# First batch's keys in three parts instead of two, scored two steps behind, and a shorter choice of its expert

## The chip, the core and the metric

The kernel runs on one core of a Trainium2 chip. The metric is the device time of one execution in microseconds (us), as the median of several runs. Five engines matter: TensorE (PE, its weight loads are PEld), VectorE (DVE), ScalarE (ACT), GpSimd (POOL) and SyncE (SP), which issues nearly all transfers. Each engine takes its instructions in the order in which the program was laid out. That layout is made when the program is compiled: a planner takes the order of the source as the order of priority and moves an instruction ahead where its inputs and its buffer are free.

## The reference

Four batches of 10048 tokens with 128 channels, 49 agents, 16 experts (4 groups of 4) with 1024 hidden units.

```python
a2k = softmax(scale * agents @ k.T)      # 49 x 10048, per batch
agent_v = a2k @ v                        # 49 x 128
x = softmax(scale * q @ agents.T) @ agent_v
g = argmax(x @ w_group); e = argmax(x @ w_expert[g])
out = p(g) * p(e | g) * (relu(x @ w1[g, e]) @ w2[g, e])
```

The values of a token depend on all keys of its batch, through `agent_v`. So no token of the first batch can go through an expert before all of that batch's keys and values have been read.

## The kernel before, in words

Keys, values and queries come in chunks of 8 tiles of 128 tokens: ten chunks to a batch, the last one of 7 tiles (the seventh of 64 rows). The program handles batch 1 first, then 2, 3 and 0 (`PB`). It has three pieces in time:

- **The front**, lines 424 to 529, runs alone before anything else. It reads the first batch's keys and values, forms `agent_v`, picks the expert that most of the batch's tokens will take (the main expert) and starts to load its weights.
- **The experts.** Lines 1239 to 1266 pass tile after tile of 512 tokens through the main expert, batch after batch. Beside them run "lanes", the same attention work for the later batches and the routing of this one, which are advanced by how far the experts have come.
- **The rest**: tokens of the last batch that take another expert are gathered, computed and scattered.

In the front the order of the work around the keys is a string, `ORDER` (line 68): `k` loads and splits the next key chunk, `m` takes the maximum over the chunks since the last `m`, `v` takes the exponentials of the next chunk and issues its value load, `q` runs the whole of query chunk 0. Scores and value products always run one step behind.

A key chunk goes like this. `load` (214) brings 512 KB into one of four `xf` buffers. `split_load` (224) makes a high half `xh` on ACT and the rest `xl` on DVE, or on POOL in four pieces where `POOLED` (69) has a 1: chunks 1, 4 and 7. Both halves come from a pool `wk` with two buffers each. `key_scores` (272) issues 24 matmuls, three for each tile of 128 keys, copies the bank to `S` on ACT and takes the maximum over the tiles from `S` on DVE (285). `key_max` (291) is a chain between two engines: reduce the chunk maxima (`mx`), transpose on PE, reduce again (`ma`), multiply into a diagonal (`dg`), spread over all partitions by a matmul with ones, copy to `mb`. `key_exp` (318) subtracts `mb` on DVE, takes the exponential on ACT and issues the value load (`vf`, six buffers). `key_values` (336) multiplies the exponentials with the values in fp32, two matmuls in the trace for each tile of 128 keys, into one PSUM bank. That bank holds one sum for each of the two parts; `agents_done` (468) scales and adds them and divides, which gives `av`.

`main_soon` (751) then chooses the main expert from the sum of the tokens: two small matmuls and eleven DVE instructions from `msum` to `mainid`. `load_weights` (812) reads `mainid` into a register of SP and issues the loads `w1f` and `w2f`. `agents_scaled` (496) scales `av` into `at`: transpose, reduction and reciprocal on one partition, and a matmul with ones that spreads the result. `at` multiplies `w1f` in `weights_of` (824), which the first expert tile needs, and makes `rh` for the routing.

```python
ORDER = "kkkkkmkvkvkvkvkvmqvvvvv"
POOLED = "0100100100"
```

Of the kernel before, what the change touches and what calls it, by code (L numbers as in the profile page):

```python
# [11 lines left out]
F16 = mybir.dt.float16  # L12
I32 = mybir.dt.int32
AF = mybir.ActivationFunctionType
ALU = mybir.AluOpType
# [5 lines left out]
P = 128  # L21
B = 4
N = 10048
C = 128
# [42 lines left out]

ORDER = "kkkkkmkvkvkvkvkvmqvvvvv"
POOLED = "0100100100"
RANGES = [(0, CT), (CT, 3 * CT), (3 * CT, 5 * CT), (5 * CT, 7 * CT), (7 * CT, NTP)]  # L70
# [62 lines left out]
def build(ctx, tc, qT, kT, v, agT, wr, w1, w2, cpk, out):  # L133
# [90 lines left out]
    def split_load(kind, b, ci, early=None):  # L224
        t0, t1 = chunks[ci]
        n = (t1 - t0) * P if kind == "q" else min(N, t1 * P) - t0 * P
        xf = loaded.pop((kind, b, ci), None)
        if xf is None:
            xf = load(kind, b, ci)
        xh = wk.tile([P, CT * P], F16, name="xh", tag="xh")  # L230
        xl = wk.tile([P, CT * P], F16, name="xl", tag="xl")
        act.activation(xh[:, 0:n], xf[:, 0:n], AF.Copy)
        if early and POOLED[ci] == "0":
            vec.tensor_sub(out=xl[:, 0:n], in0=xf[:, 0:n], in1=xh[:, 0:n])
        else:
# [35 lines left out]

    def key_scores(b, ci):

# [10 lines left out]
        act.activation(S[:, t0:t0 + full], ps[:, 0:full * NA].rearrange("p (t a) -> p t a", a=NA), AF.Copy)  # L284
        vec.tensor_reduce(out=mch[:, ci], in_=S[:, t0:t0 + full].rearrange("p t a -> p a t"), axis=AX.X, op=ALU.max)
        if t1 == NT:
# [4 lines left out]
    def key_max(b, c0, c1, early):  # L291
# [12 lines left out]
        vec.tensor_reduce(out=ma, in_=ps[0:NA, 0:P], axis=AX.X, op=ALU.max)  # L304
        dg = sm.tile([NA, NA], F32, name="dg")
        vec.tensor_scalar(out=dg, in0=identf[0:NA, 0:NA], scalar1=ma, scalar2=None, op0=ALU.mult)
        yield
        ps = bank(b)
        pe.matmul(ps[:, 0:NA], ones[0:NA, :], dg, start=True, stop=True)
        yield  # L310
        mb = sm.tile([P, 1, NA], F32, name="mb")
        vec.tensor_copy(out=mb[:, 0], in_=ps[:, 0:NA])
        if i == 0 and early:
            st["acc"] = bank(1)
        st["part"].append((c0, c1, mb, st["acc"][0:NA, i * (C + 1):(i + 1) * (C + 1)] if early else None))
        yield

    def key_exp(b, i, ci, early):

        S, mb = state[b]["S"], state[b]["part"][i][2]  # L320
        t0, t1 = chunks[ci]
        for a, z, m in ((t0, min(t1, NT - 1), P), (NT - 1, t1, LAST)):
            if z <= a:
                continue
            vec.tensor_sub(out=S[0:m, a:z], in0=S[0:m, a:z], in1=mb[0:m].broadcast_to([m, z - a, NA]))
            act.activation(S[0:m, a:z], S[0:m, a:z], AF.Exp)
        vf = early.tile([P, CT, C + 1], F32, name="vf", tag="vf", bufs=6)
        nf = min(t1, NT - 1) - t0
# [95 lines left out]
    def front(b, early, order):  # L424

        first = queries_of(b, early, [0])
        behind, part, at, done = None, {}, {"k": 0, "v": 0}, 0
        for x in order:
            if x == "q":
                yield from first  # L430
                continue
            if x == "m":
                if behind:
                    yield from behind
                behind = None
                yield from key_max(b, done, at["k"], True)
                for c in range(done, at["k"]):
                    part[c] = len(state[b]["part"]) - 1
                done = at["k"]
                continue  # L440
            c = at[x]
            at[x] += 1
            if x == "k":
                yield from key_load(b, c, early)
            else:
                yield from key_exp(b, part[c], c, early)
            if behind:
                yield from behind
            behind = key_scores(b, c) if x == "k" else key_values(b, part[c], c)
        if behind:  # L450
            yield from behind
# [16 lines left out]
    def agents_done(b, early):  # L468

        st = state[b]  # L470
        acc, *other = [x[3] for x in st["part"]]
        if other:
            n = len(st["part"])
            mm = early.tile([NA, 1], F32, name="mm")
            vec.tensor_reduce(out=mm, in_=st["ma"][:, 0:n], axis=AX.X, op=ALU.max)
            wt = early.tile([NA, n], F32, name="wt")
            vec.tensor_scalar(out=wt, in0=st["ma"][:, 0:n], scalar1=mm, scalar2=None, op0=ALU.subtract)
            act.activation(wt, wt, AF.Exp)
            a0 = early.tile([NA, C + 1], F32, name="a0")
            vec.tensor_scalar(out=a0, in0=acc, scalar1=wt[:, 0:1], scalar2=None, op0=ALU.mult)  # L480
            for i, x in enumerate(other):
                vec.scalar_tensor_tensor(out=a0, in0=x, scalar=wt[:, i + 1:i + 2], in1=a0, op0=ALU.mult, op1=ALU.add)
            acc = a0
        za = sm.tile([NA, 1], F32, name="za")
        vec.tensor_scalar(out=za, in0=acc[:, C:C + 1], scalar1=1e-9, scalar2=None, op0=ALU.add)
        vec.reciprocal(out=za, in_=za)
        av = sm.tile([NA, C], F32, name="av")
        vec.tensor_scalar(out=av, in0=acc[:, 0:C], scalar1=za, scalar2=None, op0=ALU.mult)
# [5 lines left out]
        yield from agents_scaled(b, psT[:, 0:NA])  # L494

    def agents_scaled(b, avT):
# [254 lines left out]
    def main_soon(b, early, av):  # L751

        st = state[b]
        row = lambda n, name: sm.tile([1, n], F32, name=name)
        su, g, e, o, m = row(NG + NE, "msum"), row(1, "mg"), row(1, "me"), row(NG, "mog"), row(NE, "mm")
        ps = bank(b)
# [7 lines left out]
        yield  # L764
        vec.tensor_copy(out=su, in_=ps[0:1, 0:NG + NE])
        vec.tensor_reduce(out=g, in_=su[:, 0:NG], axis=AX.X, op=ALU.max)
        vec.tensor_reduce(out=e, in_=su[:, NG:], axis=AX.X, op=ALU.min)
        vec.tensor_scalar(out=o, in0=su[:, 0:NG], scalar1=g, scalar2=None, op0=ALU.is_ge)
        vec.tensor_scalar(out=m, in0=su[:, NG:], scalar1=e, scalar2=None, op0=ALU.subtract)
        vec.tensor_mul(out=m.rearrange("p (g e) -> p g e", g=NG), in0=m.rearrange("p (g e) -> p g e", g=NG),  # L770
                       in1=o.unsqueeze(2).broadcast_to([1, NG, 4]))
        vec.tensor_reduce(out=g, in_=m, axis=AX.X, op=ALU.max)
        vec.scalar_tensor_tensor(out=m, in0=m, scalar=g, in1=rev[0:1], op0=ALU.is_ge, op1=ALU.mult)
        vec.tensor_reduce(out=g, in_=m, axis=AX.X, op=ALU.max)
        vec.tensor_scalar(out=e, in0=g, scalar1=-1.0, scalar2=float(NE - 1), op0=ALU.mult, op1=ALU.add)
        mi = sm.tile([1, 1], I32, name="mainid")
        vec.tensor_copy(out=mi, in_=e)
        st["mainid"], st["maine"] = mi, e
        yield

    def main_row(b):

        st = state[b]
        ps = bank(b)
        pe.matmul(ps[:, 0:1], ones[0:1, :], st["maine"], start=True, stop=True)
        yield
# [507 lines left out]
```

## Time and profile before

| | |
|---|---|
| median of 3 runs | 1002.93 us (998.78 to 1003.92) |
| the profiled execution's own time | 1004.48 us |
| its span, first to last instruction | 1002.6 us |
| mean granted clock of TensorE | 0.975 of full speed |
| busy: PE, DVE, ACT, POOL | 922.4, 770.3, 639.9, 474.1 us |
| read from HBM, written | 89.01 MB, 33.75 MB |

All times below are us from the span's start. Busy time of PE is the time with a matmul in the pipe, so matmuls that overlap count once. In the granted clock 1.00 stands for 2.4 GHz and 0.50 for 1.2 GHz, the two levels. In a timeline row the second number runs from the start of the first instruction of a merged row to the end of the last one; the number in brackets is the idle time before it and who ended it.

### The profile page before, as it was taken

To read this page: it belongs to the slowest core of one execution; us is meant where nothing else is said; L and a number is where in the kernel's file an instruction comes from. 1 tells how busy PE (TensorE), PEld (TensorE's weight loads), DVE (VectorE), ACT (ScalarE), POOL (GpSimd) and SP (SyncE) were. 2 spreads that over 40 slices of the span, in tenths; PEclk is the share of its full clock that TensorE was granted. 3 is DMA by queue.
4 is the path that set the end of the run, shared out by engine and by line. 5 is a ranking of instruction groups with operands and counts; after the bars stand their busy time and mean duration, and the time that the engine had idled before them with its cause. 6 is when DMAs were issued, how large, how long until landed. Compare 5 with 4: busy or idle time off the path is not lost.

```text
span 1002.6 us, 31456 instructions
## 1 busy us (share of the span) xinstructions
PE 922.4 (92%) x13192; PEld 733.5 (73%) x13192; DVE 770.3 (77%) x1477; ACT 639.9 (64%) x1144; POOL 474.1 (47%) x772
## 2 busy tenths in 40 slices
PE   3878998989998999999899989999999999999986
PEld 3756776767776777787677868877776777777765
DVE  5769879987698887868979766689998766666643
ACT  4537667688756787875677657865455655555542
POOL 2226347288304536730362255400003758888885
PEclk9879999999999999999999999999999999999988
DMA  9744236344037734301773332112422734343321
GB/s 280 231 138 132 80 103 206 95 141 120 23 118 252 203 97 124 103 24 36 240 258 107 110 96 62 33 36 75 161 70 94 251 116 157 125 125 117 117 71 43
DMA packets 104423, 124.58 MB, mean 124 GB/s; under 512 B 6743, under 2 KB 88152, under 8 KB 101328
## 3 DMA queue, kind: packets, MB, share of 16 engines
q1 hardware_dynamic: 99920, 116.57, 36.5%
q0 software_dynamic: 4352, 5.91, 2.2%
q8 instruction: 105, 1.72, 0.7%
q14 instruction: 46, 0.38, 0.1%
HBM read 89.01 MB, written 33.75 MB: 122 GB/s over the span
## 4 chain that ended last, share of the span: by engine, by line
PE 37%; DVE 13%; POOL 6%; issue 2%; ACT 2%; DMA 1%; POOLq 0%; SPq 0%; DVEq 0%; ACTq 0%
PE po L128 19%; PE ph L128 13%; DVE hl L128 6%; PE at L128 5%; POOL out L1111 2%; POOL er L1074 2%; POOL gap L1090 1%; POOL xl L238 1%; DVE oo L128 1%; DMA xf<-kT 1%; ACT hh L128 1%; DVE oh L128 1%; DVE oa L128 1%; DVE za L128 0%; ACT vh L128 0%
## 5 line engine op out<-in xcount | busy, mean ns | idle before, releaser
L128 DVE SCALAR_TENSOR_TENSOR hl<-ph,hh 128x512 f16<-128x512 f32 (+1 forms) x656 | 437.2, 678 | 143.8 <-ACT hh L128 141.0
L128 PEld LDWEIGHTS <-hh 128*128 128x128 f16 x5200 | 427.9, 98 | 150.7 <-issue 6.3
L128 ACT ACTIVATE hh<-ph 128x512 f16<-128x512 f32 (+1 forms) x656 | 382.6, 592 | 210.7 <-PE ph L128 205.4
L128 PE MATMUL po<-wbuf,hh 128*128 128x128 f16 x4816 | 476.4, 220 | 0.0
L128 PE MATMUL po<-wbuf,hl 128*128 128x128 f16 x2408 | 439.1, 220 | 0.0
L128 PE MATMUL ph<-et,wbuf 98*128 98x512 f16 (+1 forms) x1040 | 311.9, 380 | 20.9 <-DVE hl L128 20.5
L238 POOL TENSOR_TENSOR xl<-xf,xh 128x256 f16<-128x256 f32 (+1 forms) x288 | 191.9, 700 | 207.1 <-ACT xh L128 204.7
L128 PEld LDWEIGHTS <-hl 128*128 128x128 f16 x2600 | 254.9, 98 | 2.9 <-issue 0.3
L1074 POOL DMA_INDIRECT er<-erow,gidx x68 | 69.3, 1019 | 126.2 <-DVE over L128 113.1
L128 PEld LDWEIGHTS <-wbuf 98*128 98x128 f16 x1216 | 95.7, 99 | 32.4 <-issue 29.6
L128 ACT ACTIVATE xh<-xf 128x1024 f16<-128x1024 f32 x80 | 83.4, 1043 | 46.0 <-PE at L128 19.0
L380 POOL TENSOR_TENSOR sl<-S,sh 128x147 f16<-128x147 f32 (+1 forms) x90 | 46.0, 538 | 97.2 <-ACT sh L128 97.2
L1111 POOL DMA_INDIRECT out<-oo,sidx x68 | 67.7, 995 | 25.5 <-DVE oo L128 14.5
L590 POOL TENSOR_TENSOR rows<-ef,rows 128x147 f16<-128x147 f32 (+2 forms) x117 | 48.0, 437 | 50.0 <-ACT rows L128 49.8
L128 PEld LDWEIGHTS <-xh 128*128 128x128 f16 x1264 | 60.8, 100 | 14.3 <-ACT xh L128 12.8
L128 PE MATMUL at<-agh,xl 128*128 128x49 f16 x577 | 58.1, 187 | 8.8 <-POOL xl L238 8.8
L128 PEld LDWEIGHTS <-xl 128*128 128x128 f16 x632 | 53.3, 99 | 14.4 <-POOL xl L238 11.3
L128 PE MATMUL at<-agh,xh 128*128 128x49 f16 x577 | 58.3, 187 | 2.2 <-ACT xh L128 2.0
L128 PE MATMUL at<-agl,xh 128*128 128x49 f16 x577 | 57.9, 187 | 0.0
L128 PE MATMUL ph<-ets,wbuf 98*128 98x512 f16 x176 | 53.6, 388 | 0.0
L1090 POOL MEMSET gap<- 128x320 f16 x136 | 52.3, 384 | 0.3
L128 DVE TENSOR_TENSOR oo<-po,cw 128x512 f32<-128x512 f32 x65 | 43.7, 673 | 10.1 <-PE po L128 10.1
(281 smaller groups left out, 1061.5 us busy)
## 6 DMA issues: line engine op xcount, KB each, us to landing
xf<-kT SPq DMA_DIRECT2D x36, 512.0 KB, 4.3
vf<-v SPq DMA_DIRECT2D x36, 512.0 KB, 5.2
xf<-qT SPq DMA_DIRECT2D x36, 512.0 KB, 4.1
out<-oo SPq DMA_DIRECT2D x62, 256.0 KB, 2.5
wbuf<-wall SPq DMA_DIRECT2D x11, 1024.0 KB, 5.0
wsg<-wall SPq DMA_DIRECT2D x6, 1024.0 KB, 5.0
erow<-rows SPq DMA_DIRECT2D x3, 1975.0 KB, 7.7
w1f<-w SPq DMA_DIRECT2D x7, 512.0 KB, 5.5
```

The costliest lines, as they stand in the source:

```text
L128: return f(*a, **k)
L238: pool.tensor_sub(out=xl[:, y], in0=xf[:, y], in1=xh[:, y])
L380: pool.tensor_sub(out=sl[0:m, w], in0=x[:, j], in1=sh[0:m, w])
L590: (vec if early else pool).tensor_sub(out=rows[:, w, NA:2 * NA], in0=ef[:, y], in1=rows[:, w, 0:NA])
L1074: ins = pool.indirect_dma_start(out=er[:, q], out_offset=None, in_=erow[b][:, :], in_offset=bass.IndirectOffsetOnAxis(ap=place(b, j * w + ...
L1090: tc.keep_in_program_order(pool.memset(gap, 0.0))
L1111: ins = pool.indirect_dma_start(out=out, out_offset=bass.IndirectOffsetOnAxis(ap=place(x["b"], x["j"] * n + q)[1], axis=0), in_=o[:, q], i ...
```

## The change

`ORDER` becomes a list of sixty steps with separate letters for loading a key chunk (`l`), splitting it (`k`), scoring it (`s`), loading values (`V`), exponentials (`v`), products (`p`), loading the queries (`Q`) and one stage of query chunk 0 (`q`). Scores stand two splits behind. There are three `m`, after chunks 3, 6 and 9. Each step also advances the running maximum by one stage. Odd key chunks split into a second pair of buffers, and POOL splits chunks 1, 3, 6 and 8. The maximum of the tiles is read from PSUM. The third part's sum has a PSUM bank of its own. In `key_max` and in `agents_scaled` a matmul with a broadcast operand takes the place of the diagonal and of the one-partition step. The choice of the expert takes five DVE instructions and writes the index by `max_index`; the first reduction of `agents_scaled` is held behind it.

```diff
-ORDER = "kkkkkmkvkvkvkvkvmqvvvvv"
-POOLED = "0100100100"
+ORDER = ("l l l l k l k l k l s V k l s V k l s V k l s m k Q s V v s V v p s V v p m V k v p s V k p v s V k p v s V p m v p "
+         "v p q v p v p q q q").split()
+POOLED = "0101001010"
@@ split_load
-        xh = wk.tile([P, CT * P], F16, name="xh", tag="xh")
-        xl = wk.tile([P, CT * P], F16, name="xl", tag="xl")
+        xp = early if early and kind == "k" and ci % 2 else wk
+        xh, xl = [xp.tile([P, CT * P], F16, name=x, tag=x, bufs=2) for x in ("xh", "xl")]
@@ key_scores
-        vec.tensor_reduce(out=mch[:, ci], in_=S[:, t0:t0 + full].rearrange("p t a -> p a t"), axis=AX.X, op=ALU.max)
+        x = ps[:, 0:full * NA].rearrange("p (t a) -> p t a", a=NA) if early else S[:, t0:t0 + full]
+        vec.tensor_reduce(out=mch[:, ci], in_=x.rearrange("p t a -> p a t"), axis=AX.X, op=ALU.max)
@@ key_max
-        dg = sm.tile([NA, NA], F32, name="dg")
-        vec.tensor_scalar(out=dg, in0=identf[0:NA, 0:NA], scalar1=ma, scalar2=None, op0=ALU.mult)
         yield
         ps = bank(b)
-        pe.matmul(ps[:, 0:NA], ones[0:NA, :], dg, start=True, stop=True)
+        pe.matmul(ps[:, 0:NA], ma.broadcast_to([NA, P]), identf[0:NA, 0:NA], start=True, stop=True)
...
-        if i == 0 and early:
+        if early and i != 1:
             st["acc"] = bank(1)
-        st["part"].append((c0, c1, mb, st["acc"][0:NA, i * (C + 1):(i + 1) * (C + 1)] if early else None))
+        k = i % 2 * (C + 1)
+        st["part"].append((c0, c1, mb, st["acc"][0:NA, k:k + C + 1] if early else None))
@@ front
+        query = queries_of(b, early, [0])
+        next(query)
+        chain, part, at = iter(()), {}, dict.fromkeys("lksmVvp", 0)
...
         for x in order:
+            next(chain, None)
...
+            elif x == "m":
+                whole(chain)
+                chain = key_max(b, c and at["done"], at["s"], early)
+                for y in range(c and at["done"], at["s"]):
+                    part[y] = c
+                at["done"] = at["s"]
+                next(chain)
+            elif x == "V":
+                yield from key_values_load(b, c, early)
+            elif x == "v":
+                if part[c] >= len(st["part"]):
+                    whole(chain)
+                yield from key_exp(b, part[c], c)
+            elif x == "p":
+                yield from key_values(b, part[c], c)
+        whole(query)
@@ agents_scaled
-        vec.tensor_reduce(out=am, in_=avT, axis=AX.X, op=ALU.max, apply_absolute_value=True)
+        ins = vec.tensor_reduce(out=am, in_=avT, axis=AX.X, op=ALU.max, apply_absolute_value=True)
+        if pinned:
+            tc.keep_in_program_order(ins)
         yield
         ps = bank(b)
-        pe.transpose(ps[0:1, 0:P], am, identf)
-        yield
-        sc = sm.tile([1, 2], F32, name="sc")
-        vec.tensor_reduce(out=sc[:, 1:2], in_=ps[0:1, 0:P], axis=AX.X, op=ALU.max)
-        vec.tensor_scalar(out=sc[:, 1:2], in0=sc[:, 1:2], scalar1=1e-30, scalar2=1.0 / AMAX, op0=ALU.max, op1=ALU.mult)
-        vec.reciprocal(out=sc[:, 0:1], in_=sc[:, 1:2])
-        yield
-        ps = bank(b)
-        pe.matmul(ps[:, 0:2], ones[0:1, :], sc, start=True, stop=True)
+        pe.matmul(ps[:, 0:P], am.broadcast_to([P, P]), identf, start=True, stop=True)
         yield
         scb = sm.tile([P, 2], F32, name="scb")
-        vec.tensor_copy(out=scb, in_=ps[:, 0:2])
+        vec.tensor_reduce(out=scb[:, 1:2], in_=ps[:, 0:P], axis=AX.X, op=ALU.max)
+        vec.tensor_scalar(out=scb[:, 1:2], in0=scb[:, 1:2], scalar1=1e-30, scalar2=1.0 / AMAX, op0=ALU.max, op1=ALU.mult)
+        vec.reciprocal(out=scb[:, 0:1], in_=scb[:, 1:2])
@@ main_soon, in place of the eleven instructions of lines 765 to 777
+        g, o, m = row(1, "mg"), row(NG, "mog"), row(NE, "mm")
+        vec.tensor_reduce(out=g, in_=ps[0:1, 0:NG], axis=AX.X, op=ALU.max)
+        vec.tensor_scalar(out=o, in0=ps[0:1, 0:NG], scalar1=g, scalar2=1.0, op0=ALU.is_ge, op1=ALU.subtract)
+        vec.scalar_tensor_tensor(out=m.rearrange("p (g e) -> p g e", g=NG), in0=o.unsqueeze(2).broadcast_to([1, NG, 4]), scalar=3e38,
+                                 in1=ps[0:1, NG:NG + NE].rearrange("p (g e) -> p g e", g=NG), op0=ALU.mult, op1=ALU.add)
+        best = row(8, "best")
+        which = sm.tile([1, 8], U32, name="which")
+        vec.max(out=best, in_=m)
+        vec.max_index(out=which, in_max=best, in_values=m)
+        st["mainid"] = which.bitcast(I32)
```

`agents_done` adds three parts in the place of two, by one more DVE instruction of the kind at line 482; `key_values_load` is the second half of `key_exp` (lines 327 to 334) as a step of its own; `main_row` casts the index back to a float.

## Rows read from the trace of the kernel before

**Rows 1.** Busy time by stage: stretch, length, PE, PEld, DVE, ACT, POOL, clock, DMA, GB/s
```profile
0.00:63.00 63.00, 41.29 (x478) 36.53 (x479) 35.14 (x99) 25.08 (x40) 15.14 (x25) 0.93 0.67 204
...
83.00:100.00 17.00, 14.66 (x199) 11.40 (x198) 16.84 (x45) 11.80 (x24) 9.54 (x18) 1.00 0.39 123
...
300.00:400.00 100.00, 94.11 (x1451) 75.02 (x1449) 83.28 (x137) 76.37 (x135) 50.82 (x85) 0.98 0.56 169
```

**Rows 2.** Timeline of ACT, 0 to 62: splits, what each waited for
```profile
11.06 1.06 ACT L128 ACTIVATE xh<-xf 128x1024 f16<-128x1024 f32 x1 [1.23 <-PE po L128]
...
24.24 1.06 ACT L128 ACTIVATE xh<-xf 128x1024 f16<-128x1024 f32 x1 [3.59 <-PE ph L128]
25.20 0.48 ACT L128 ACTIVATE S<-ph 128x392 f32<-128x392 f32 x1
...
32.92 0.90 ACT L128 ACTIVATE xh<-xf 128x832 f16<-128x832 f32 x1 [2.02 <-PE at L128]
```

**Rows 3.** Timeline of PE, 24 to 58: value products, maximum, query chunk 0
```profile
26.26 5.80 PE L128 MATMUL at<-vf,S 128*49 128x129 f32 x32 [0.81 <-ACT S L128]
...
32.70 1.97 PE L128 MATMUL at<-vf,S 128*49 128x129 f32 x16
...
40.15 0.31 PE L128 MATMUL at<-cp,mx 128*49 128x128 f32 x1 [0.31 <-DVE mx L128]
...
43.35 0.87 PE L128 MATMUL at<-vf,S 128*49 128x129 f32 x6 [1.70 <-ACT S L128]
44.06 1.34 PE L128 MATMUL ph<-ones,ef 128*49 128x1 f32 x16
...
49.01 7.92 PE L128 MATMUL at<-vf,S 128*49 128x129 f32 x60
```

**Rows 4.** Timeline of DVE, 22 to 62: both maxima, agents, choice of expert
```profile
22.16 0.57 DVE L128 TENSOR_REDUCE mx<-mch 128x49 f32<-128x245 f32 x1
...
23.60 0.24 DVE L128 TENSOR_SCALAR dg<-cp,ma 49x49 f32<-49x49 f32 x1
...
24.83 0.21 DVE L128 COPY mb<-at 128x49 f32<-128x49 f32 x1 [0.97 <-PE at L128]
...
29.05 0.81 DVE L128 TENSOR_REDUCE mch<-S 128x49 f32<-128x392 f32 x1
...
30.28 1.21 DVE L128 TENSOR_TENSOR xl<-xf,xh 128x1024 f16<-128x1024 f32 x1
...
39.52 0.57 DVE L128 TENSOR_REDUCE mx<-mch 128x49 f32<-128x245 f32 x1
...
56.97 0.34 DVE L128 TENSOR_SCALAR a<-at,wt 49x129 f32<-49x129 f32 x1 [7.43 <-PE at L128]
...
59.37 0.17 DVE L128 COPY msum<-po 1x20 f32<-1x20 f32 x1
...
61.62 0.13 DVE L128 CAST mainid<-me 1x1 int32<-1x1 f32 x1
```

**Rows 5.** Busy time, 39 to 51: the second maximum and the products behind it
```profile
39.00:44.00 5.00, 2.92 (x41) 2.38 (x40) 4.19 (x13) 1.43 (x4) 0.16 (x1) 1.00 0.91 283
44.00:51.00 7.00, 7.00 (x48) 6.33 (x47) 2.97 (x7) 4.10 (x8) 3.87 (x6) 0.51 0.20 77
```

**Rows 6.** Busy time by 5 us: stretch, length, PE, PEld, DVE, ACT, POOL, clock, DMA, GB/s
```profile
25.00:30.00 5.00, 4.19 (x29) 3.90 (x27) 4.96 (x8) 4.13 (x8) 3.28 (x4) 1.00 1.11 338
```

**Rows 7.** Timeline of POOL, 0 to 44: key chunks split in four pieces
```profile
9.92 2.56 POOL L238 TENSOR_TENSOR xl<-xf,xh 128x256 f16<-128x256 f32 x4 [9.47 <-ACT xh L128]
...
25.43 3.28 POOL L238 TENSOR_TENSOR xl<-xf,xh 128x256 f16<-128x256 f32 x4 [6.84 <-ACT xh L128]
```

**Rows 8.** DMA issues, 0 to 64: operation, count, KB each, median us to landing
```profile
xf<-kT SPq DMA_DIRECT2D x9, 512.0 KB, 6.5
```

**Rows 9.** Timeline of SP, 0 to 120: the first key loads
```profile
2.20 1.85 SPq L219 DMA_DIRECT2D xf<-kT  x4
```

**Rows 10.** Timeline of PE, 56 to 76: weights of the main expert
```profile
67.30 3.75 PE L128 MATMUL at<-w1f,at 128*128 128x512 f32 x4 [1.94 <-DMA w1f<-w]
```

More of the change, by code (lines that the diff above doesn't have):

```diff
@@ L13 @@
 I32 = mybir.dt.int32
+U32 = mybir.dt.uint32
 AF = mybir.ActivationFunctionType
@@ L270, in load_only, with key_scores @@
         yield
-    def key_scores(b, ci):
+    def key_scores(b, ci, early=None):
         st = state[b]
@@ L312, in key_max, with key_exp @@
         vec.tensor_copy(out=mb[:, 0], in_=ps[:, 0:NA])
-        if i == 0 and early:
+        if early and i != 1:
             st["acc"] = bank(1)
-        st["part"].append((c0, c1, mb, st["acc"][0:NA, i * (C + 1):(i + 1) * (C + 1)] if early else None))
+        k = i % 2 * (C + 1)
+        st["part"].append((c0, c1, mb, st["acc"][0:NA, k:k + C + 1] if early else None))
         yield
-    def key_exp(b, i, ci, early):
+    def key_exp(b, i, ci):
         S, mb = state[b]["S"], state[b]["part"][i][2]
@@ L326, in key_exp, with key_values_load @@
             act.activation(S[0:m, a:z], S[0:m, a:z], AF.Exp)
+        yield
+    def key_values_load(b, ci, early):
+        t0, t1 = chunks[ci]
         vf = early.tile([P, CT, C + 1], F32, name="vf", tag="vf", bufs=6)
@@ L424, in front, with whole @@
     def front(b, early, order):
-        first = queries_of(b, early, [0])
-        behind, part, at, done = None, {}, {"k": 0, "v": 0}, 0
+        st = state[b]
+        st["part"] = []
+        query = queries_of(b, early, [0])
+        next(query)
+        chain, part, at = iter(()), {}, dict.fromkeys("lksmVvp", 0)
+        def whole(gen):
+            for _ in gen:
+                pass
         for x in order:
+            next(chain, None)
+            if x == "Q":
+                yield from load_only("q", b, 0)
+                continue
             if x == "q":
[L430 to L439, printed above, removed]
+                for y in query:
+                    if y == "chunk":
+                        break
                 continue
@@ L442, in front @@
             at[x] += 1
-            if x == "k":
+            if x == "l":
+                yield from load_only("k", b, c)
+            elif x == "k":
                 yield from key_load(b, c, early)
[L445 to L451, printed above, removed]
+            elif x == "s":
+                yield from key_scores(b, c, early)
+            elif x == "m":
[14 more added lines that the diff above has]
+        whole(query)
         for ci in range(1, 4):
@@ L470, in agents_done @@
         st = state[b]
[L471 to L483, printed above, removed]
+        acc = [x[3] for x in st["part"]]
+        n = len(acc)
+        mm = early.tile([NA, 1], F32, name="mm")
+        vec.tensor_reduce(out=mm, in_=st["ma"][:, 0:n], axis=AX.X, op=ALU.max)
+        wt = early.tile([NA, n], F32, name="wt")
+        vec.tensor_scalar(out=wt, in0=st["ma"][:, 0:n], scalar1=mm, scalar2=None, op0=ALU.subtract)
+        act.activation(wt, wt, AF.Exp)
+        a0 = early.tile([NA, C + 1], F32, name="a0")
+        vec.tensor_scalar(out=a0, in0=acc[0], scalar1=wt[:, 0:1], scalar2=None, op0=ALU.mult)
+        for i in range(1, n):
+            vec.scalar_tensor_tensor(out=a0, in0=acc[i], scalar=wt[:, i:i + 1], in1=a0, op0=ALU.mult, op1=ALU.add)
         za = sm.tile([NA, 1], F32, name="za")
-        vec.tensor_scalar(out=za, in0=acc[:, C:C + 1], scalar1=1e-9, scalar2=None, op0=ALU.add)
+        vec.tensor_scalar(out=za, in0=a0[:, C:C + 1], scalar1=1e-9, scalar2=None, op0=ALU.add)
         vec.reciprocal(out=za, in_=za)
         av = sm.tile([NA, C], F32, name="av")
-        vec.tensor_scalar(out=av, in0=acc[:, 0:C], scalar1=za, scalar2=None, op0=ALU.mult)
+        vec.tensor_scalar(out=av, in0=a0[:, 0:C], scalar1=za, scalar2=None, op0=ALU.mult)
         yield
@@ L493, in agents_done, with agents_scaled @@
         pe.transpose(psT[:, 0:NA], av, identf[0:NA, 0:NA])
-        yield from agents_scaled(b, psT[:, 0:NA])
-    def agents_scaled(b, avT):
+        yield from agents_scaled(b, psT[:, 0:NA], True)
+    def agents_scaled(b, avT, pinned=False):
         st = state[b]
         am = sm.tile([P, 1], F32, name="am")
-        vec.tensor_reduce(out=am, in_=avT, axis=AX.X, op=ALU.max, apply_absolute_value=True)
+        ins = vec.tensor_reduce(out=am, in_=avT, axis=AX.X, op=ALU.max, apply_absolute_value=True)
+        if pinned:
+            tc.keep_in_program_order(ins)
         yield
         ps = bank(b)
-        pe.transpose(ps[0:1, 0:P], am, identf)
-        yield
-        sc = sm.tile([1, 2], F32, name="sc")
-        vec.tensor_reduce(out=sc[:, 1:2], in_=ps[0:1, 0:P], axis=AX.X, op=ALU.max)
-        vec.tensor_scalar(out=sc[:, 1:2], in0=sc[:, 1:2], scalar1=1e-30, scalar2=1.0 / AMAX, op0=ALU.max, op1=ALU.mult)
-        vec.reciprocal(out=sc[:, 0:1], in_=sc[:, 1:2])
-        yield
-        ps = bank(b)
-        pe.matmul(ps[:, 0:2], ones[0:1, :], sc, start=True, stop=True)
+        pe.matmul(ps[:, 0:P], am.broadcast_to([P, P]), identf, start=True, stop=True)
         yield
         scb = sm.tile([P, 2], F32, name="scb")
-        vec.tensor_copy(out=scb, in_=ps[:, 0:2])
+        vec.tensor_reduce(out=scb[:, 1:2], in_=ps[:, 0:P], axis=AX.X, op=ALU.max)
+        vec.tensor_scalar(out=scb[:, 1:2], in0=scb[:, 1:2], scalar1=1e-30, scalar2=1.0 / AMAX, op0=ALU.max, op1=ALU.mult)
+        vec.reciprocal(out=scb[:, 0:1], in_=scb[:, 1:2])
         at = const.tile([P, P], F32, name=f"at2{b}")
@@ L754, in main_soon @@
         row = lambda n, name: sm.tile([1, n], F32, name=name)
-        su, g, e, o, m = row(NG + NE, "msum"), row(1, "mg"), row(1, "me"), row(NG, "mog"), row(NE, "mm")
         ps = bank(b)
@@ L764, in main_soon @@
         yield
[L765 to L778, printed above, removed]
+        g, o, m = row(1, "mg"), row(NG, "mog"), row(NE, "mm")
[8 more added lines that the diff above has]
+        st["mainid"] = which.bitcast(I32)
         yield
@@ L783, in main_row @@
         st = state[b]
+        e = sm.tile([1, 1], F32, name="me")
+        vec.tensor_copy(out=e, in_=st["mainid"][:, 0:1])
         ps = bank(b)
-        pe.matmul(ps[:, 0:1], ones[0:1, :], st["maine"], start=True, stop=True)
+        pe.matmul(ps[:, 0:1], ones[0:1, :], e, start=True, stop=True)
         yield
```

## The prediction, made before the changed kernel ran

> **What bounds the kernel now.** I read the busy time by stage first, because the change touches only the front. From 100 on TensorE is the bound: it is busy 94 of every 100 us or so, and VectorE carries 83 [rows 1]. In the first 63 us it has a matmul in the pipe for only 41 of them [rows 1]. So the front is a stage with a limit of its own, and what it gives up should come off the end: all the work behind it starts that much earlier.
>
> Inside the front I went through the timelines, ScalarE first. From the third on the splits of the keys don't wait for keys. The third waits for the matmuls of an earlier chunk to give back a split buffer, and so do later ones, the last at 32.92 [rows 2]. Then TensorE. The products with the values begin at 26.26, when the first maximum is through, and run to 49.01 + 7.92 = 56.93; VectorE stands idle for 7.43 us until they are done [rows 3, 4]. So products end the front, and two things hold them up. They start late. And at the second maximum they break off: TensorE idles 2.08 of 5 us, and then the granted clock is 0.51 for 7 us, the lower of its two levels [rows 5].
>
> The pace of the products: 32 matmuls (16 tiles) took 5.80 us in the first group, 0.362 a tile; 16 took 1.97 in the next, 0.246 a tile [rows 3]. Between these two rows lies one chunk's scores, 0.64 us. The clock column reads 1.00 there [rows 6], yet the first group runs at the slow pace, so I count the first 5.7 us of products as slow, whenever they begin.
>
> **The change, part by part.**
>
> *Start of the products.* Part one now needs four key chunks, not five, and the odd chunks have split buffers of their own. Chunk 1's rest ends on POOL at 12.48 [rows 7], chunk 3's follows there: 15.1. Its scores could be done at 15.3, copy and maximum of the chunk 0.48 and 0.81 later [rows 2, 4]: 16.5. But its copy may stand on ScalarE behind the split of chunk 5. That chunk takes chunk 1's buffer at 12.5; by the median of 6.5 us it would land at 19.0 [rows 8]. The 4.1 MB issued up to it (constants, six key chunks, one of values) take 12.0 us at 338 GB/s [rows 6] from 2.2, when the first key load is issued [rows 9]: 14.2. I take 16.2, nearer the second, as little is queued ahead of it. Split to 17.3, copy 17.8, then on VectorE the rest of chunk 5 (1.21) and the maximum (0.81) [rows 4]: mx starts near 19.2. From mx to mb took 22.16 to 25.04; without dg (0.24) it is 2.64. From mb to the first product it took 1.22 [rows 3, 4]. So the first product starts at 23.1, not 26.26. Ends: 20.4 if the copy isn't held up; 26.26 if nothing is won. I take 23.0.
>
> *What then runs on TensorE.* Slow to 28.7: one chunk's scores at the slow pace (0.96) and 13 tiles of products. Left are 79 - 13 = 66 tiles, 16.2 us; scores of three key chunks and of query chunk 0, 2.6; the TensorE steps of two maxima, 0.7 each by the row of 0.31 and about as much for the second matmul, 1.4; the sums over query chunk 0, 1.34 [rows 3], and some 1.0 for its transposes (an estimate by the same row). These now come last in the order and may fall into the idle time behind the products: half of them, 1.2. End: 28.7 + 16.2 + 2.6 + 1.4 + 1.2 = 50.1. **Gain 6.8 us.**
>
> *Is the transfer in time, and do the two later maxima break the products off?* Ahead of the last key chunk go constants (0.4 MB), ten key chunks and about four of values: 7.6 MB, which at 338 GB/s from 2.2 on is 24.7. Split, rest, scores, copy and maximum add 4.2, the chain and the exponentials 3.9: 32.8. By then TensorE has done about 25 of the 56 tiles of parts one and two; 31 tiles are 7.6 us of work in front of it, twice the 3.83 us from mx to product of the second maximum before [rows 3, 4]. So there is cover. If it is gone, a maximum costs what it costs now. The last values (11.2 MB) land near 35, ahead of their turn. The queue of SP: value loads wait only from the seventh on, for a buffer of the first products, and by then all key loads are issued.
>
> *The maximum read from PSUM.* The trace shows no VectorE read beside ScalarE's copy of the same bank, so the gain lies between 0 and the copy's 0.48 us [rows 2] for each of three chains; I take 0, as the copy stands first in the source. The Trainium skill (PSUM — Partial Sum Buffer, section on bank collisions) speaks against this edit: two engines that touch the same bank and partitions at once raise an error, two reads included, so they are kept apart. No run here shows that. By it the sum stands as it is; without it the first product would be 0.5 earlier.
>
> *A fourth key chunk on POOL* takes 1.21 us off VectorE [rows 4]. But a POOL split took 3.28 us beside busy VectorE and 2.56 beside an idle one [rows 7], so both slow down together; I cost it at 0, covered by VectorE's wait for the products, and at up to 0.7 on the start if that cover is gone. The Trainium skill (SBUF — State Buffer, "Who interferes with whom") says that a VectorE instruction with two SBUF inputs contends with a GpSimd instruction that reads SBUF; the trace agrees, by 0.72 us here. By that rule the saving of 1.2 is given back, without it the chunk would be free.
>
> *Three sums.* One more addition of 0.34, but the first two can be done while part three runs. On the path one instruction stands where two stood: gain 0.4 [rows 4].
>
> *Choice of the expert.* From msum to the end of mainid went 59.37 to 61.75, 2.38 us for eleven instructions with others between [rows 4]. Five dependent ones at 0.2 are 1.0; the trace has no max or max_index, each between 0.13 and 0.34 by the nearest short rows: 1.0 to 1.4 in all, gain 1.0 to 1.4. TensorE does wait for the weights that this releases (1.94 us idle until w1f) [rows 10], so it lies on the path. Against it: the scaling of the agents now begins only behind the choice, about 0.5 us later than now as seen from av, in spite of the shorter steps (an estimate: 0.2 for each of five steps, less what one round over TensorE cost), and what hangs on it is VectorE work, 16.84 of 17 us busy from 83 on [rows 1]. I take 0.7, ends -0.5 and 1.2. The shorter steps in the later batches' lanes I cost at nothing: TensorE's expert matmuls hide them; uncovered they are under a microsecond a batch. The buffers of the new pair are free long before the expert stage takes their place.
>
> **Sum:** 6.8 + 0.4 + 0.7 = 7.9 us. The profiled execution took 1004.48, 1.55 above the median; 996.6 for it, and 995.0 against the median of 1002.93.
>
> **Rivals.**
> - *One maximum still breaks the products off.* For it: the order on each engine is fixed when the program is laid out, not when data come; the second maximum shows the price, 2.08 us idle plus 7.0 us at the slow pace, 7.0 x (1 - 0.246/0.362) = 2.2. Against it: the cover of 31 tiles. 7.9 - 4.3 = 3.6: 999.3.
> - *The chains are the bound: slower.* Every small step of a maximum stands on VectorE and TensorE behind later chunks' splits. At the first it eats the earlier start (3.2); at the second and third TensorE has nothing else and pays 3.83 + 2.2 = 6.0 each. 15.2 against 7.9: 1010.2. Three chains in place of two make it worse; it decides from the point where the products queued behind a chain are fewer than 16 tiles. The backlog speaks against it.
> - *More than I take.* The copy isn't held up (2.6 more), the choice gives all (0.5): 991.9; with the query work behind the products, 990.7.
> - *The new order isn't what runs.* The planner already moves work past the order of the source; if it lays out nearly the same queues, 1003.
>
> **Chances.** Forecast 0.48, its own range 992.9 to 996.9; more 0.17; one break 0.26; chains 0.06; same queues 0.03. A measurement of this kernel can tell about 0.5%, 5 us, from no change. Faster by more: nearly all of the forecast, all of "more", a little of the break: 0.68. Within: 0.26. Slower: 0.06. The range reaches from 989.7 over the break's time to 1001.0.
>
> **What would show it.** First product near 23; no idle time over 1 us in TensorE from there to the end of the products near 50, and clock 1.00 from about 29 on; splits that wait for keys, not for matmuls; msum's place to mainid in about 1.2 us; w1f's matmul about 8 us earlier than 67.3; the same busy shares behind it. Wrong would be products that end past 53, a clock of 0.5 among them, or an early end of the front that the last instruction doesn't show.

## The result and the profile after

Median 992.09 us (four runs, 990.50 to 993.12) against 1003.42 for the kernel before on the same chip (four, 998.78 to 1006.98): a ratio of 0.9888 [0.9845, 0.9932], that is 7 to 16 us. The profiled execution took 992.58, its span is 990.7. The range held the result. The forecast was 995.0; its own narrower range, 992.9 to 996.9, ends 0.8 above it.

The busy time of the engines, from the page, and the clock row of the 40 slices: the same number of matmuls as before within one, in less time.

```profile
PE 916.1 (92%) x13191; PEld 729.3 (74%) x13191; DVE 762.4 (77%) x1467; ACT 640.0 (65%) x1144; POOL 477.9 (48%) x776
...
PEclk9979999999999999999989999999999999999998
```

Busy time by stage, columns as in [rows 1]:

```profile
0.00:63.00 63.00, 44.83 (x537) 38.32 (x538) 35.77 (x114) 28.90 (x48) 22.71 (x38) 0.92 0.79 244
...
39.00:44.00 5.00, 4.12 (x52) 3.46 (x50) 2.59 (x9) 0.90 (x3) 0.00 (x0) 1.00 0.90 304
44.00:51.00 7.00, 6.71 (x70) 6.18 (x70) 2.82 (x10) 3.69 (x7) 4.61 (x8) 1.00 0.05 22
50.00:55.00 5.00, 2.81 (x37) 2.32 (x37) 2.80 (x17) 0.60 (x1) 1.99 (x4) 0.71 0.01 3
```

Where 39 to 51 held an idle TensorE and then 7 us at the lower clock level [rows 5], it is now busy for 10.83 of 12 us at 1.00. The clock falls only behind the products (0.71 from 50 to 55), where TensorE is busy for 2.81 of 5 us.

The timeline of PE, 23 to 60:

```profile
23.64 5.93 PE L130 MATMUL at<-vf,S 128*49 128x129 f32 x32
29.50 0.31 PE L130 MATMUL at<-cp,mx 128*49 128x128 f32 x1
...
34.31 5.50 PE L130 MATMUL at<-vf,S 128*49 128x129 f32 x48
39.74 0.31 PE L130 MATMUL at<-cp,mx 128*49 128x128 f32 x1
39.98 1.97 PE L130 MATMUL at<-vf,S 128*49 128x129 f32 x16
...
43.89 5.42 PE L130 MATMUL at<-vf,S 128*49 128x129 f32 x46 [0.88 <-ACT S L130]
49.24 0.89 PE L130 MATMUL at<-ones,ef 128*49 128x1 f32 x16
...
58.60 0.55 PE L130 MATMUL po<-rh,et 98*128 98x21 f16 x15 [1.13 <-DVE rh L130]
59.00 3.61 PE L130 MATMUL at<-w1f,at 128*128 128x512 f32 x4
```

The transposes of both later maxima (29.50, 39.74) stand among products and cost their own 0.31. The products run from 23.64 to 49.31; before, from 26.26 to 56.93 [rows 3]. The third maximum still leaves a gap, 0.88. `w1f`'s matmul starts at 59.00, 8.3 earlier [rows 10]. What it waits for has changed: `w1f` landed at 58.32 (4.1 after its issue), and TensorE stood until 58.60 waiting for `rh`, which comes from the scaling of the agents.

The timeline of ACT, the first splits (against [rows 2]):

```profile
8.49 1.06 ACT L130 ACTIVATE xh<-xf 128x1024 f16<-128x1024 f32 x1 [0.52 <-DMA xf<-kT]
9.74 1.06 ACT L130 ACTIVATE xh<-xf 128x1024 f16<-128x1024 f32 x1 [0.18 <-DMA xf<-kT]
11.10 1.06 ACT L130 ACTIVATE xh<-xf 128x1024 f16<-128x1024 f32 x1 [0.30 <-DMA xf<-kT]
12.06 0.48 ACT L130 ACTIVATE S<-po 128x392 f32<-128x392 f32 x1
```

The splits wait for keys, no longer for matmuls. The timeline of POOL, chunks 1 and 3:

```profile
9.64 6.08 POOL L240 TENSOR_TENSOR xl<-xf,xh 128x256 f16<-128x256 f32 x8 [9.19 <-ACT xh L130]
```

The timeline of DVE around the first maximum and from the products' end to the choice:

```profile
12.57 0.57 DVE L130 TENSOR_REDUCE mch<-po 128x49 f32<-128x392 f32 x1 [0.52 <-ACT S L130]
...
17.29 0.49 DVE L130 TENSOR_REDUCE mx<-mch 128x49 f32<-128x196 f32 x1
...
20.18 0.19 DVE L130 COPY mb<-ph 128x49 f32<-128x49 f32 x1
...
49.35 0.35 DVE L130 SCALAR_TENSOR_TENSOR a<-at,wt,a 49x129 f32<-49x129 f32 x1 [2.28 <-PE at L130]
50.17 0.15 DVE L130 COPY se<-at 49x1 f32<-49x1 f32 x1 [0.48 <-PE at L130]
...
50.75 0.43 DVE L130 COPY et<-po 98x512 f16<-98x512 f16 x1 [0.18 <-PE po L130]
51.09 0.35 DVE L130 TENSOR_SCALAR av<-a,za 49x128 f32<-49x128 f32 x1
...
52.39 0.15 DVE L130 TENSOR_REDUCE mg<-ph 1x1 f32<-1x4 f32 x1 [0.32 <-PE ph L130]
...
53.29 0.15 DVE L130 FIND_INDEX8 which<-best,mm 1x8 uint32<-1x16 f32 x1
```

The maximum takes 0.57 from PSUM where it took 0.81 from `S`, but starts at 12.57, behind ACT's copy of that bank (12.06 to 12.54). `av` is done 2.13 after the last product, where it took 1.45. The choice takes 1.05, from 52.39 to 53.44, where it took 2.38.

Landmarks, read from the timelines (us). "First rows" is the DVE instruction `oo` of the first expert tile, "58th" that of the 58th.

| | first product | products end | `av` done | `w1f` issued | its matmul | first rows | 58th | span |
|---|---|---|---|---|---|---|---|---|
| before | 26.26 | 56.9 | 58.4 | 62.5 | 67.3 | 93.8 | 776.0 | 1002.6 |
| after | 23.64 | 49.3 | 51.4 | 54.2 | 59.0 | 85.7 | 766.1 | 990.7 |
| gain | 2.6 | 7.6 | 6.9 | 8.3 | 8.3 | 8.1 | 9.9 | 11.9 |

### The profile page after: what moved, and what is told of

Read it like the earlier page. It is cut to its first block, busy times and chain, and to the rows that moved or that the text cites. A ratio compares the mean times of both kernels' runs of the same rounds, so it can differ in the third digit from the quotient of the medians.

```text
span 990.7 us, 31434 instructions
## 1 busy us (share of the span) xinstructions
PE 916.1 (92%) x13191; PEld 729.3 (74%) x13191; DVE 762.4 (77%) x1467; ACT 640.0 (65%) x1144; POOL 477.9 (48%) x776
## 4 chain that ended last, share of the span: by engine, by line
PE 34%; DVE 13%; POOL 6%; DMA 3%; issue 2%; ACT 2%; SPq 0%; POOLq 0%; DVEq 0%; ACTq 0%
PE po L130 17%; PE ph L130 12%; DVE hl L130 6%; PE at L130 5%; POOL out L1127 3%; DMA xf<-kT 2%; POOL gap L1106 1%; DVE oo L130 1%; POOL er L1090 1%; ACT hh L130 1%; DMA w1f<-w 1%; DMA er<-erow,gidx 1%; POOL xl L240 1%; DVE oh L130 1%; DVE oa L130 1%
## 5 line engine op out<-in xcount | busy, mean ns | idle before, releaser
L240 POOL TENSOR_TENSOR xl<-xf,xh 128x256 f16<-128x256 f32 x292 | 196.6, 706 | 200.2 <-ACT xh L130 187.1
L130 PEld LDWEIGHTS <-xl 128*128 128x128 f16 x632 | 53.0, 99 | 14.1 <-POOL xl L240 12.4
```

Source lines behind the costliest of these rows:

```text
L130: return f(*a, **k)
```

## The experiments

All times are told against the kernel before on the same chip. The changed kernel again, the two parts, the one pair of buffers and the long choice ran on one chip (before 1037.25); the kernel before again, the buffers alone, the query work and the first string for `POOLED` on a second (1036.77); the other three strings on a third (1014.52). Each run has one trace. Differences in landmarks are against the second trace of the changed kernel; for the strings, against its first ("as changed").

**The changed kernel again**, unchanged.

> The changed kernel again, unedited. The lead over the kernel before was 8.1 us at the first expert tile's rows and 11.9 at the end. Theory (the 3.8 us that came later are chance of these two executions): the time at the first tile's rows comes back within 0.5 us of 85.7, while the stretch from there to the last tile's rows differs by 1 to 4 us from the 896.0 of the first execution. Rival (they come from the order of the work behind the front, laid out anew): the stretch comes back within 0.7 us.

1028.82, 0.9919 [0.9888, 0.9951]. First product 23.33, products' end 49.35, first rows 85.88, 58th 765.96: all within 0.31 us of the first trace, in an execution 36 us longer. To the 58th tile the stretch comes back within 0.3 (680.1 against 680.3), as the rival had it; between, the two traces are up to 3.3 apart (the 15th tile) and come together again, with the same order of instructions on VectorE. The whole difference lies behind 770 us, in the last batch. Instruction groups of VectorE from 770 to the end, of the first trace and then of this one (idle time before them, and what ended it, behind the second bar):

```profile
L130 DVE SCALAR_TENSOR_TENSOR hl<-ph,hh 128x512 f16<-128x512 f32 (+1 forms) x179 | 122.3, 688 | 68.9 <-ACT hh L130 68.6
```

```profile
L130 DVE SCALAR_TENSOR_TENSOR hl<-ph,hh 128x512 f16<-128x512 f32 (+1 forms) x181 | 122.7, 686 | 104.3 <-ACT hh L130 70.9 <-issue 24.5 <-ACT ets L130 7.2
```

The work and its durations are equal; of the 35.4 us of new idle time, 24.5 are time in which the engine waits for nothing that the profile shows, and 7.2 a wait for ACT. The cause of both is open. The kernel before is slower here as well (1037.25), so across chips only the landmarks of the front and the ratios to the kernel before can be compared.

**The kernel before again.** Between the 41st and the 42nd tile's rows it loses 18.38 us, the changed kernel 16.17; is that the order or the occasion?

> The kernel before, unedited. Its first execution took 18.4 us between the rows of the 41st and 42nd expert tile (582.1 to 600.5), the changed kernel 16.2, and the two executions of the changed kernel agree at 42 to 58 within 0.3 us in their lead. Theory (chance of that one execution of before): the first tile's rows come back within 0.5 us of 93.8, the 18.4 us come back as 16 to 17. Rival (the order in which the kernel before was laid out loses it each time): 18 to 19 again.

18.38 again, as the rival had it, but the first rows came at 92.64, 1.2 earlier. The changed kernel's second trace has 17.7 at this place, and the edited ones 17.3 to 17.7, so its 16.17 was the occasion and the two orders differ by some 0.7. The front of the kernel before varies more than that of the changed one: its products ended at 55.92, 1.0 earlier than in the first trace, and its 58th rows came at 772.5, 3.5 earlier. Between this trace and the changed kernel's second one, on another chip, the lead is 6.6 at the products' end, 6.8 at the first rows and 6.6 at the 58th, against 7.6, 8.1 and 9.9 in the first pair.

**The middle maximum taken out**: two parts of 4 and 6 chunks. The exponentials and products of chunk 4 and the later ones have to move behind the last maximum; all else is as changed.

```diff
-... s V v p m V k v p s V k p v s V k p v s V p m v p v p q v p v p q q q
+... s V v p V k v p s V k p s V k s V m v p v p v p q v p v p v p q q q
```

> The changed kernel with the middle maximum taken out: part one is chunks 0 to 3, part two chunks 4 to 9, no value product of chunk 4 or later before the last maximum. Theory (the middle maximum keeps TensorE fed): the 32 tiles of part one are done near 33, TensorE then waits for the last maximum near 40, the granted clock falls to 0.50 behind the break, and the products end 4 to 6 us later than in the changed kernel (49.3): 53 to 55; whole time 4 to 6 us above the changed kernel. Rival (the earlier start alone gives the gain, the last maximum sets the end anyway): products end within 1.5 us of 49.3, whole time within 2 us.

1035.14, 0.9977 [0.9955, 0.9998], which is 6.3 above the changed kernel on this chip. First product 23.69 (0.4 later), products' end 53.59 (4.2 later), first rows 92.80 (6.9 later; where the other 2.7 are lost was not followed). Busy time by 5 us, columns as in [rows 1]:

```profile
35.00:40.00 5.00, 1.88 (x32) 1.37 (x29) 4.00 (x16) 0.57 (x3) 0.00 (x0) 0.86 1.10 290
40.00:45.00 5.00, 4.57 (x22) 4.38 (x23) 3.26 (x8) 5.00 (x10) 1.24 (x3) 0.50 0.62 245
45.00:50.00 5.00, 5.00 (x45) 4.98 (x44) 0.00 (x0) 0.15 (x1) 4.37 (x7) 0.95 0.00 0
```

This is [rows 5] again: 3.1 us idle, then the lower level. A maximum in the middle is what keeps products in TensorE's queue.

**One pair of split buffers.** `xp = wk` for all chunks.

> The changed kernel with one pair of split buffers for all chunks instead of two. Theory (from the third chunk on the splits waited for buffers): splits wait for matmuls again, first product 1 to 3 us later than 23.6, end of products 1 to 3 us later than 49.3, whole time as much. Rival (the split is early enough either way): first product and end of products within 0.7 us.

1033.75, 0.9964 [0.9940, 0.9987], which is 4.9 above the changed kernel. First product 26.74 (3.4 later), products' end 53.05 (3.7 later), first rows 91.16 (5.3 later): the theory's way, and more than it said. The timeline of ACT has the old waits back:

```profile
10.71 1.06 ACT L130 ACTIVATE xh<-xf 128x1024 f16<-128x1024 f32 x1 [1.23 <-PE po L130]
...
23.15 1.06 ACT L130 ACTIVATE xh<-xf 128x1024 f16<-128x1024 f32 x1 [3.93 <-PE at L130]
```

**The buffers alone**, in the kernel before.

```diff
-        xh = wk.tile([P, CT * P], F16, name="xh", tag="xh")
-        xl = wk.tile([P, CT * P], F16, name="xl", tag="xl")
+        xp = early if early and kind == "k" and ci % 2 else wk
+        xh, xl = [xp.tile([P, CT * P], F16, name=x, tag=x, bufs=2) for x in ("xh", "xl")]
```

> The kernel before with the second pair of split buffers for odd key chunks, nothing else. Theory (the buffers only pay with scores two steps behind and three parts): splits stop waiting for matmuls, first product 0 to 1 us earlier than 26.26, the break at the second maximum stays, first expert tile's rows within 1 us of 93.8. Rival (the buffers alone bring the earlier start): first product 2 to 3 us earlier, end of products and first rows 2 us earlier or more.

1040.20, 1.0037 [1.0019, 1.0055]: slower by 0.4%, which neither expectation had. First product 29.26, 3.0 later than in the kernel before, first rows 95.96, 2.2 and 3.3 later than in its two traces. Timeline of POOL, then of DVE:

```profile
9.64 4.55 POOL L238 TENSOR_TENSOR xl<-xf,xh 128x256 f16<-128x256 f32 x4 [9.19 <-ACT xh L128]
```

```profile
10.83 2.83 DVE L128 TENSOR_TENSOR xl<-xf,xh 128x1024 f16<-128x1024 f32 x2 [1.74 <-ACT xh L128]
...
24.74 0.60 DVE L128 TENSOR_REDUCE mx<-mch 128x49 f32<-128x245 f32 x1
```

Freed from the matmuls, the splits crowd: VectorE takes two rests in a row, and POOL's rest of chunk 1 beside them takes 4.55, not 2.56 [rows 7]. The copies of scores on ACT come later for it, and behind them in ACT's order the split of chunk 4 (17.03 against 14.71), which is POOL's next. `mx` comes 2.6 later than in [rows 4]. The buffers paid only together with the new order.

**The long choice**: the eleven instructions of before from `msum` to `mainid`.

> The changed kernel with the old choice of the expert, eleven instructions, the scaling still held behind it. Theory (the choice lies on the path): first product and end of products as in the changed kernel (23.6, 49.3), the issue of w1f 1.2 to 1.6 us later than 54.23, the first expert tile's rows 1.2 to 1.6 us later than 85.7. Rival (it is hidden behind the rest): issue later, the first expert tile's rows within 0.4 us.

1029.29, 0.9915 [0.9884, 0.9945]. From `av`'s end to the issue of `w1f` 3.65 us, against 2.79. The first rows come at 86.72, 0.84 later, though the products had ended 0.5 earlier (48.81). The timeline of DVE, the chain's two ends:

```profile
51.89 0.17 DVE L130 COPY msum<-ph 1x20 f32<-1x20 f32 x1 [0.32 <-PE ph L130]
...
53.67 0.14 DVE L130 CAST mainid<-me 1x1 int32<-1x1 f32 x1
```

1.92 us against 1.05: the shorter choice is worth 0.86 up to the issue of `w1f`. Counted from `av`, the first rows come 1.4 later; why more than 0.86 was not followed. At the 58th rows this trace is 1.2 ahead (764.7), and 0.5 on the whole time can't be told apart, so no gain is shown behind the front.

**The query work behind `av`**, so that `se` and `et` don't stand ahead of it on VectorE.

```diff
-... v p q v p v p q q q
+... v p q v p v q p
@@ agents_done(b, early, query), behind av
+        for y in query:
+            if y == "chunk":
+                break
@@ behind load_weights
+        for y in query:
+            pass
@@ stages of query chunk 0
-            groups = [stages[:2]] + [[x] for x in stages[2:]]
+            groups = [stages[:2], stages[2:3], [query_sums]] + [[x] for x in stages[3:]]
```

> The changed kernel with the sums over query chunk 0 placed behind the division that gives av, and its split and transposes behind the choice of the expert. In the changed kernel av ends 2.13 us after the last product, 1.45 in the kernel before, because the copies of se and et stand between the steps on VectorE. Theory (that order costs 0.7 to 1.0 us on the path): av, w1f and the first expert tile's rows 0.6 to 1.0 us earlier. Rival (what is pushed back is needed just as soon): av earlier, first rows within 0.3 us or later.

1028.57, 0.9919 [0.9897, 0.9941]. `av` 0.1 earlier, but `w1f` is issued 1.35 later and the first rows come 2.5 later than in the second trace of the changed kernel; the whole time is not told apart. The timeline of DVE:

```profile
52.60 0.43 DVE L130 COPY et<-ph 98x512 f16<-98x512 f16 x1 [0.44 <-PE ph L130]
...
54.66 0.16 DVE L130 FIND_INDEX8 which<-best,mm 1x8 uint32<-1x16 f32 x1
```

The planner put the copy, and then steps of the scaling of the agents (`scb`), between the steps of the choice. The work was moved, not removed.

**Which chunks POOL splits**, four strings for `POOLED`; the change has `"0101001010"` (chunks 1, 3, 6, 8).

```diff
+POOLED = "0100101010"
```

> The changed kernel with the rest of chunk 3 on VectorE in place of POOL, which had chunks 1 and 3 one behind the other until 15.72. Theory (TensorE is full from the first product on, so the start sets the end): rest of chunk 3 done near 13.5, first product 1.5 to 2.5 us earlier than 23.6, end of products and the first expert tile's rows 1 to 2.5 us earlier. Rival (VectorE takes on 1.2 us and the later keys come no earlier, so it is given back): end of products and first rows within 0.5 us.

The edit does more than this says: chunk 3 goes to VectorE and chunk 4 to POOL. 1028.69, 0.9941 [0.9913, 0.9970], and the first product at 26.68, 3.0 later: neither expectation. POOL's chunk 1 takes 4.56 here too, beside two rests in a row on VectorE; but `mb` is copied at 20.99, only 0.8 later than as changed. Most of the delay lies behind it. Chunk 4's scores wait for POOL's pieces, the split of chunk 6 stands on ACT behind their copy, POOL begins chunk 6 at 23.00 and not at 19.57, and TensorE stands at its pieces just ahead of the first product. The timeline of POOL, then of PE:

```profile
23.00 3.35 POOL L240 TENSOR_TENSOR xl<-xf,xh 128x256 f16<-128x256 f32 x4 [2.29 <-ACT xh L130]
```

```profile
25.78 0.22 PE L130 MATMUL po<-agh,xl 128*128 128x49 f16 x1 [0.52 <-POOL xl L240]
...
26.41 0.22 PE L130 MATMUL po<-agh,xl 128*128 128x49 f16 x1 [0.20 <-POOL xl L240]
...
26.68 5.45 PE L130 MATMUL at<-vf,S 128*49 128x129 f32 x32
```

To part the two, chunk 4 back on VectorE:

```diff
+POOLED = "0100001010"
```

> The changed kernel with POOL taking the rest of key chunks 1, 6 and 8, in place of 1, 3, 6 and 8. The run with 1, 4, 6 and 8 had its first product at 26.7: chunk 1's rest on POOL took 4.6 us beside two rests in a row on VectorE, and later TensorE stood at chunk 4's pieces. Theory (both cost, the second more): mx near 17.8 as in that run, TensorE no longer held by chunk 4, first product 23 to 24.5, end of products and first expert tile's rows within 1 us of the changed kernel (49.3, 85.8). Rival (the late start comes from chunk 3 on VectorE alone): first product past 26 again.

1004.59, 0.9905 [0.9873, 0.9937]. Chunk 1 still takes 4.57 on POOL, yet the first product is at 24.16, the products' end at 48.72, the first rows at 85.63: as changed, within 0.6. So chunk 4's pieces were what cost, and chunk 3 may go to either engine: with it on POOL or not, the first rows differ by 0.1.

None on POOL in part one, then none at all:

```diff
+POOLED = "0000001010"
+POOLED = "0000000000"
```

> The changed kernel with POOL taking the rest of key chunks 6 and 8 alone, so that VectorE and POOL never split at the same time in part one. Theory (VectorE and POOL hold each other up; in part one that sets the first maximum, and the start of the products sets their end): every rest of chunks 0 to 3 takes 1.2 us, mx near 15 (17.3 in the changed kernel), first product 20.5 to 22 (23.6), end of products and first expert tile's rows 1.5 to 3 us earlier. Rival (landing of the keys and the later chunks set the end): mx earlier, but end of products and first rows within 0.7 us.

> The changed kernel with no key chunk on POOL. Theory (as for the run with 6 and 8, and TensorE also waits for POOL's pieces of chunks 6 and 8, 2.6 us in all in the changed kernel): first product 20 to 22, first rows 0.3 to 1.5 us earlier than with 6 and 8 on POOL. Rival (VectorE becomes the bound with two rests more, 2.4 us): end of products and first rows 1 to 2.5 us later than with 6 and 8 on POOL.

1002.93, 0.9892 [0.9861, 0.9922], and 999.97, 0.9872 [0.9837, 0.9907]. Products end at 47.72 and 46.69 (1.6 and 2.6 earlier than as changed), first rows 83.62 and 83.71 (2.1 and 2.0 earlier). The first of the two met its theory at the end, not at the start; in the second the products end 1.0 earlier than in the first, but the first rows don't, which neither expectation had. The first products come at 22.70 and 23.29, later than expected. The timeline of DVE of the second says why:

```profile
15.88 0.49 DVE L130 TENSOR_REDUCE mx<-mch 128x49 f32<-128x196 f32 x1
16.28 2.35 DVE L130 TENSOR_TENSOR xl<-xf,xh 128x1024 f16<-128x1024 f32 x2
18.57 0.28 DVE L130 TENSOR_REDUCE ma<-at 49x1 f32<-49x128 f32 x1
...
20.96 1.23 DVE L130 TENSOR_TENSOR xl<-xf,xh 128x1024 f16<-128x1024 f32 x1
22.12 0.55 DVE L130 TENSOR_TENSOR S<-S,mb 128x392 f32<-128x392 f32 x1
```

`mx` is 1.4 earlier than as changed, but `ma` stands behind two rests and the subtraction behind a third. What is won is behind that: the first 32 products take 4.23 us, not 5.93. That is 1.7 of the 2.6 us at the products' end, and it goes with the clock, which rises to its upper level at 24.3 and not at 28.2 (last section). No run tells whether POOL's missing pieces brought the clock up, or the occasion: in two executions of the kernel before the first 32 products took 5.80 and 6.63. With no key chunk of the front on POOL (the string holds for the front alone; POOL's later work stays) the kernel has its best ratio, and its front is 2 us shorter than as changed, in one trace; the ratios 0.9872 and 0.9888, on two chips, overlap.

## Why the prediction was right, and where it was off

- **The frame held.** The front gives up time and the end comes earlier. At the first rows the lead is 8.1 in one pair of traces and 6.8 in the other; by the medians the whole gained 11.3 in the first runs and 8.4 on the chip where the changed kernel ran again; 7.9 was forecast. In the first pair 3.8 of 11.9 came behind the front, where the lead wanders between 6.1 and 10.5. That needs no cause in the change: two traces of one kernel differ by up to 3.3 (after) and 3.7 (before) over the same tiles, and the second pair shows no such growth (6.8, then 6.6).
- **The maxima keep out of the products' way.** This was the forecast against the rival "one maximum breaks the products off", and the runs show it: without the middle one the break is back with its price (4.3 by the rival's sum, 4.2 measured at the products' end). The backlog decided. 0.88 of idle time stayed at the third.
- **Start of the products: right sum (23.0, measured 23.64), wrong terms.** I had the copy held up behind a split, `mx` near 19.2. The copies went ahead of the splits, and `mx` came at 17.29. But from `mx` to the end of `mb` I took 2.64, and it took 3.08; from there to the first product I took 1.22, and it took 3.27: the exponential stood on ACT behind two copies of scores until 22.20, and the product on PE behind chunk 6's scores, which waited for POOL's pieces (0.38 and 0.20). The errors nearly cancelled, which is luck.
- **The slow first products: right time, wrong reason.** I read the 5.80 us of the first 32 as one slow pace and counted 5.7 us of it "whenever they begin", to 28.7. The row mixes two paces: 20 products 0.21 apart, then the rest 0.11 apart from 30.5 on. As changed the pace rose at 28.2, without POOL at 24.3 after five products. It goes with the clock, not with the number of products; that 28.7 came near is luck.
- **The end of the products: 50.1 predicted, 49.3 measured; gain 6.8, measured 7.6, and 6.6 in the second pair.** The query sums that I had half ahead of it all fell behind it (49.24).
- **Three sums: +0.4 predicted, 0.7 lost.** I counted additions and not the queue: `se` waits for the query sums and `et` for transposes, and both stand ahead of `av` on VectorE. That `av` came 0.1 earlier without them (its own row took 0.83 there) leaves open how much an order could win back.
- **The choice: 1.0 to 1.4 less, net 0.7 predicted.** The chain itself gave 0.87 against the long one in the new order (1.92 less 1.05), and 0.86 reached the issue of `w1f`. But it is on the path for another reason than the one I gave: TensorE no longer waits for `w1f` there but for `rh`, as the scaling is held behind the choice. From `av` to the issue of `w1f` the two kernels differ by 1.37; the other 0.5 was already there with the long choice, in the new order.
- **The maximum from PSUM: 0, right for the wait.** The Trainium skill (PSUM — Partial Sum Buffer, section on bank collisions) has two engines kept apart on one bank; the trace agrees: the reduction starts 0.03 after ACT's copy ends, by a wait for ACT. The reduction itself got shorter by 0.24, which I had not counted.
- **A fourth chunk on POOL: 0, near, with a wrong reason.** With three chunks (1, 6 and 8) the products end 0.6 earlier and the first rows come 0.1 earlier. I named VectorE's wait for the products as the cover. It isn't one in the first 25 us, where POOL's pieces stand ahead of TensorE's next work. The Trainium skill (SBUF — State Buffer, "Who interferes with whom") spoke against this edit; the trace agrees: a chunk took 3.04 on POOL as changed (6.08 for two), and 4.55 to 4.57 beside two VectorE subtractions in a row, against 2.56 beside an idle VectorE.
- **The clock** was at 1.00 from 28.2 to the products' end, and the splits waited for keys, as said.

No run takes the scores back to one step behind, or the maximum from PSUM or the broadcast operands by themselves, so their shares are not shown.

## What to carry to other kernels

Find the stage that has a limit of its own and count the work queued beside each dependent chain: a reduction over many chunks is free as long as other products stand ready in the matmul queue, and splitting it into more parts can be what puts them there. Cost a helper engine by who waits for its pieces in order, not by its idle time. Before a lead is put down to the order of the work, see how far two traces of one kernel lie apart. When a buffer is added, ask what will crowd once the wait is gone: alone it made this kernel slower.

## What was not expected of the hardware

- A POOL subtraction of four 128x256 pieces took 2.56 us beside a VectorE that stood idle until 12.15 [rows 7], and 4.55 to 4.57 beside two VectorE subtractions in a row, in three kernels; the VectorE pair took 2.83 to 2.84 then and 2.34 to 2.35 alone.
- The clock column counts time without a record of the clock as 1.00. As changed the first record begins at 28.2 us; the column reads 1.00 ahead of it, yet a value product began every 0.21 us until then and every 0.11 from then on. The trace without POOL has records from 14.1 on: 0.50 from 17.5 to 24.3, then 1.00, and its pace changes at 24.3 by the same step. So the 1.00 of [rows 6] is no reading either: the first record there is at 30.5, where the pace rose. Busy time of the matmuls and loads that read or write `vf` (PE, PEld, DVE, ACT, clock, DMA, GB/s), without POOL in the front, then as changed:

```profile
23.30:24.30 1.00, 1.00 (x5) 0.97 (x6) 0.00 (x0) 0.00 (x0) 0.50 1.09 396
24.50:27.40 2.90, 2.90 (x28) 2.77 (x25) 0.07 (x1) 0.00 (x0) 1.00 1.12 331
```

```profile
23.70:28.10 4.40, 4.40 (x21) 4.22 (x22) 0.06 (x1) 0.00 (x0) 1.00 1.06 332
28.30:29.40 1.10, 1.10 (x12) 1.02 (x10) 0.00 (x0) 0.00 (x0) 1.00 1.21 291
```

- `max_index` shows as two instructions, 0.08 and 0.15 us on 16 elements.
- The same kernel took 992 and 1029 us on two chips, all of the difference in the last quarter of the span. The cause is open.
